# Decays of two tiles: bias inside a 128-row spreading product, exponentials of 512 columns

## The chip, the core and the metric

The kernel runs on one core of a Trainium2 chip. The core has a matmul engine (TensorE, PE in the profile), an elementwise engine (VectorE, DVE), an activation engine (ScalarE, ACT), a general one (GpSimd, POOL) and a queue engine that issues transfers (SyncE, SP). The metric is the device time in microseconds (us) of one execution. Before the change three runs took 531.83, 534.07 and 534.23 us; the median is 534.07.

## The reference, cut to what matters

Three layers follow one another on 4 batches of 768 positions. The first is a chunked linear attention with decays; its output feeds a gated feed-forward of width 1536 with RMS normalisation, and that one a second feed-forward of width 1024 with a shift by one position and a sigmoid gate.

```python
log_a = np.log(np.clip(a, 1e-06, 1.0))
for c in range(nc):
    cum = np.cumsum(la, axis=-1)
    L = np.exp(cum[:, :, :, None] - cum[:, :, None, :]) * causal
    CB = np.einsum('bhin,bhjn->bhij', Cc, Bc)
    y_intra = np.einsum('bhij,bhjd->bhid', CB * L, xc)
    y_inter = np.einsum('bhin,bhnd->bhid', Cc, state) * np.exp(cum)[..., None]
    state = decay_full * state + sum_j(B_j x_j decay_from_j)
...
xn = x / np.sqrt(np.mean(x * x, axis=-1, keepdims=True) + 1e-06) * rms_g
x = (silu(xn @ w_gate) * (xn @ w_val)) @ w_out
...
k = np.maximum(xk @ w_k, 0.0)
out = sigmoid(xr @ w_r) * ((k * k) @ w_v)
```

The matrix `L` is the "decays" of the title: for each batch and head a triangle of exponentials of differences of running sums of logarithms.

## The kernel before, in words

The sequence is cut into 6 tiles of 128 positions; with the 4 batches a tile has T = 512 columns. For each tile the kernel does the attention (8 heads, in chunks of 128 instead of 32), the normalisation, the first feed-forward (`ffn1`, 12 units of 128 channels, each with a gate product `g`, a value product `v` and, two units later, the contraction `x`) and the second one (`ffn2`, 8 units). A fp32 product is made of three products of rounded parts (`mm3`), so a unit of `ffn1` has 12 products before its contraction. The attention of tile t+1 is woven into the units of tile t by `hook`; that of tile 0 stands alone at the start, the prologue.

The weights come as 8-byte numbers and are turned into high and low parts on the chip, in pairs of jobs: ACT scales the two halves of the words (L257, L258), DVE clamps, merges twice and subtracts (L262, L267, L269, L279), and ACT rounds (L278). The first two pairs are converted in the prologue, the others among the units of tiles 0 and 1, from transfers into two staging buffers (`wst`).

Decays of tiles 0 and 1 are made by `sums_e`, `spread_e` and `exp_e`. `sums_e` takes the logarithm of `a` in 16 rows of 512 columns, sums along them with restarts (`starts`), keeps the rounded part and the rest as 32 + 32 rows of `sums`, and by four small products with `pick` brings the same sums into columns, with the sign turned (`cum`). For each batch and half (4 heads), `spread_e` makes in a PSUM tile `Eb` the sum of two products: an identity times a triangle of zeros and -30000 (`before`), and a row of `sums`, picked and spread over the 128 partitions. `exp_e` then takes four exponentials of 128 columns, each with its column of `cum` as the bias. Decays of the later tiles are made by scans over a loaded, spread copy of `a` (`load_e`, `e_scan`).

In the prologue, for each batch: `scores` makes the products of B and C in two PSUM tiles, `mask` multiplies them with the decays on DVE (`M`), `y_mm` makes the output and the state. After four batches the normalisation follows in two halves of columns (`rms_a`, `rms_b`, `xn_f`, `xn_split`), and with it the first products of `ffn1` can start. `decays` writes the clipped `a` to memory, twice, for the loads of later tiles.

The order in which each engine gets its instructions is not that of the code. The class `Order` takes all instructions with their dependences, holds a price for each kind, and lists them engine by engine in the order in which it would start them; this order is then fixed. A change in one place can therefore shift instructions on every engine. `WARM` sets two rows of products without use that keep PE busy (L749).

PE's products for the spread of a tile-1 batch go into the two buffers of the pool `at`, those of tile 0 into the four buffers of the pool `mm`, which `ffn1` uses as well for `g` and `v`. All exponentials of tile 1 stand before the table load for SiLU.

Of the kernel before, what the change touches and what calls it, by code (L numbers as in the profile page):

```python
# [16 lines left out]
P = 128  # L17
# [8 lines left out]
KW = 16  # L26
# [26 lines left out]
def shape_constants():  # L53
# [14 lines left out]
def tile_kernel(ctx: ExitStack, tc, a_c, x_t, B_t, B_s, C_s, B_p, C_p, C_h, kc,  # L68
# [73 lines left out]
    nc.gpsimd.memset(f32(pick), 0.0)
    for base in (0, -32):
        nc.gpsimd.affine_select(out=pick, in_=f32(pick), pattern=[[-1, RE]], base=base, channel_multiplier=1,
                                compare_op=ALU.not_equal, fill=1.0)
# [8 lines left out]
    cmask = wp.tile([P, NH * P], BF16, name="cmask")  # L154
    nc.gpsimd.memset(cmask, 0.0)
    nc.gpsimd.affine_select(out=cmask, in_=cmask, pattern=[[0, NH], [1, P]], base=0, channel_multiplier=-1,
                            compare_op=ALU.not_equal, fill=1.0)
    lmask = wp.tile([P, NB, P + 1], BF16, name="lmask")
    nc.gpsimd.memset(lmask, 0.0)
    nc.gpsimd.memset(lmask[:, :, 0:1], 1.0)  # L160

# [14 lines left out]


# [149 lines left out]
    sums = wp.tile([P, T], F32R, name="sums")  # L327
    cum = wp.tile([P, 4, RE], F32, name="cum")
    wp.tile([P, 48], F32, name="pad_m")

    def sums_e(a_sb):
        nc.vector.memset(f32(sums), 0.0)
        ln = t2("ln")[:RE]
        tabled(out=ln, in_=a_sb[:RE], func=AF.Ln)
        nc.vector.tensor_tensor_scan(out=ln, data0=starts.rearrange("p h i -> p (h i)"), data1=ln, initial=0.0,
                                     op0=ALU.mult, op1=ALU.add)
        nc.vector.tensor_copy(sums[:RE], ln)
        nc.vector.tensor_tensor(out=sums[32:32 + RE], in0=ln, in1=f32(sums[:RE]), op=ALU.subtract)
        ps = patt.tile([P, T], F32, tag="at", name="cumt")[:, :4 * RE].rearrange("p (h r) -> p h r", h=4)
        for h in range(4):  # L340
            mm = nc.tensor.matmul(ps[:, h], sums[:, h * P:(h + 1) * P], pick, start=True, stop=True)
# [428 lines left out]
    for b in range(NB):  # L770
# [14 lines left out]
        if b == 0:  # L785
            decays(a_sb)
# [390 lines left out]
```

## Time and profile before

| | |
|---|---|
| time, three runs | 531.83, 534.07, 534.23 us |
| span of the profiled execution | 532.1 us, 7505 instructions |
| its own time | listed nowhere apart from the three runs above |
| PE busy | 517.5 us (97%), 2831 products |
| DVE busy | 402.7 us (76%), 640 instructions |
| ACT busy | 314.7 us (59%), 546 instructions |
| POOL busy | 14.3 us (3%), 30 instructions |
| granted TensorE clock, mean | 0.994 of full speed |

The busy shares are means over the whole span. The prologue, up to about 31 us, and the units of tiles 0 and 1, up to about 150 us, have other limits than the rest, so the views by stretch and the rows in order of time are of more use than the table. A row of a timeline gives the start, the length, the line, and in brackets how long the engine had been idle before and what ended that. Instructions that follow each other overlap a little, so the distance of two starts is the time that one costs its engine.

### The profile page before, as it was taken

Reading aid. Unit: us, or ns where it says so; the run is one execution under the profiler, and the core shown is the slowest. Engines: PE = TensorE matmul, PEld = TensorE weight load, DVE = VectorE, ACT = ScalarE, POOL = GpSimd, SP = SyncE. Lnnn points to the kernel's source line nnn. Section 1 sums busy time; section 2 is a strip of 40 time slices with the busy share of each in tenths; the row PEclk is TensorE's granted clock in tenths of the full one; section 3 lists DMA queues with packets and bytes.
Section 4 is the critical chain, followed back from the end, with each engine's and each line's share of the span. In section 5 each row is a group of like instructions: output and inputs, shape, how many; then the busy total and the mean of one; then the engine's idle time right before and its main releaser. Section 6 shows DMA issues by size and latency. Waiting matters only on the chain.

```text
span 532.1 us, 7505 instructions
## 1 busy us (share of the span) xinstructions
PE 517.5 (97%) x2831; PEld 414.7 (78%) x2831; DVE 402.7 (76%) x640; ACT 314.7 (59%) x546; POOL 14.3 (3%) x30
## 2 busy tenths in 40 slices
PE   9969989999989999999999999999999999999997
PEld 6646767778768888888788888888888888888885
DVE  5798999999999986587996598986455863335772
ACT  4998768845736774445774445774437663245552
POOL 4000000000002000001000001000000000000000
PEclk9988999999999999999999999999999999999999
DMA  8543565534334011314011314011000010000001
GB/s 256 196 158 112 172 216 183 173 94 149 99 109 149 20 41 41 118 62 176 22 39 42 119 58 160 1 41 39 1 0 2 2 39 1 0 0 1 21 21 39
DMA packets 21635, 42.20 MB, mean 79 GB/s; under 512 B 2064, under 2 KB 4880, under 8 KB 21600
## 3 DMA queue, kind: packets, MB, share of 16 engines
q1 hardware_dynamic: 19296, 33.34, 18.8%
q10 hardware_dynamic: 2304, 8.39, 4.7%
q8 instruction: 22, 0.36, 0.3%
q14 instruction: 13, 0.11, 0.1%
HBM read 38.38 MB, written 3.34 MB: 78 GB/s over the span
## 4 chain that ended last, share of the span: by engine, by line
PE 89%; DVE 2%; ACT 2%; DMA 1%; issue 1%; ACTq 0%; DVEq 0%
PE v L625 10%; PE v L627 10%; PE v L626 10%; PE g L625 7%; PE g L626 6%; PE x L627 6%; PE g L627 6%; PE x L625 6%; PE x L626 6%; PE kp L625 4%; PE kp L627 4%; PE kp L626 4%; PE y L494 2%; PE y L523 1%; PE sc L462 1%; PE rps L626 1%
## 5 line engine op out<-in xcount | busy, mean ns | idle before, releaser
L656 DVE TENSOR_TENSOR hf<-sl,v 128x512 f32<-128x512 f32 x72 | 49.2, 683 | 48.8 <-PE v L627 45.2
L128 ACT CAST h<-hf 128x512 fp32r<-128x512 f32 x72 | 44.5, 618 | 62.7 <-DVE hf L656 58.5
L116 ACT ACTIVATE sl<-g 128x512 f32<-128x512 f32 x72 | 42.7, 593 | 44.5 <-PE g L627 44.4
L131 DVE TENSOR_TENSOR h<-hf,h 128x512 fp32r<-128x512 f32 x72 | 50.4, 702 | 23.4 <-ACT h L128 23.3
L625 PE MATMUL g<-xn,wgh 128*128 128x512 f32 x144 | 58.4, 409 | 1.5 <-ACT sl L116 0.8
L625 PE MATMUL x<-h,woh 128*128 128x512 f32 x144 | 56.5, 393 | 0.8 <-ACT h L128 0.8
L626 PE MATMUL g<-xn,wgl 128*128 128x512 f32 x144 | 57.2, 397 | 0.0
L625 PE MATMUL v<-xn,wvh 128*128 128x512 f32 x144 | 56.4, 395 | 0.6 <-ACT sl L116 0.6
L627 PE MATMUL g<-xn,wgh 128*128 128x512 f32 x144 | 56.9, 395 | 0.0
L626 PE MATMUL v<-xn,wvl 128*128 128x512 f32 x144 | 56.5, 392 | 0.0
L627 PE MATMUL v<-xn,wvh 128*128 128x512 f32 x144 | 56.3, 391 | 0.0
L627 PE MATMUL x<-h,woh 128*128 128x512 f32 x144 | 55.8, 391 | 0.4 <-DVE h L131 0.4
L626 PE MATMUL x<-h,wol 128*128 128x512 f32 x144 | 56.1, 389 | 0.0
L722 DVE TENSOR_TENSOR k<-rl 128x512 f32<-128x512 f32 x48 | 35.2, 738 | 15.1 <-ACT rl L721 14.9
L128 ACT CAST h<-k 128x512 fp32r<-128x512 f32 x48 | 29.7, 620 | 16.0 <-DVE k L722 15.9
L131 DVE TENSOR_TENSOR h<-k,h 128x512 fp32r<-128x512 f32 x48 | 32.7, 685 | 7.4 <-ACT h L128 7.0
L721 ACT ACTIVATE rl<-kp 128x512 f32<-128x512 f32 x48 | 28.4, 595 | 16.2 <-PE kp L627 15.8
L625 PE MATMUL kp<-xm,wkh 128*128 128x512 f32 x96 | 37.8, 393 | 0.0
L627 PE MATMUL v<-h,wvvh 128*128 128x512 f32 x96 | 37.5, 390 | 0.0
L627 PE MATMUL kp<-xm,wkh 128*128 128x512 f32 x96 | 37.5, 390 | 0.0
L625 PE MATMUL v<-h,wvvh 128*128 128x512 f32 x96 | 37.4, 389 | 0.0
L626 PE MATMUL v<-h,wvvl 128*128 128x512 f32 x96 | 37.4, 389 | 0.0
(135 smaller groups left out, 1040.7 us busy)
## 6 DMA issues: line engine op xcount, KB each, us to landing
E<-la_r ACTq DMA_DIRECT2D x16, 512.0 KB
x<-in_x_t SPq DMA_DIRECT2D x6, 512.0 KB
wst<-in_w_gate SPq DMA_DIRECT2D x6, 512.0 KB
wst<-in_w_val SPq DMA_DIRECT2D x6, 512.0 KB
wst<-in_w_out SPq DMA_DIRECT2D x6, 512.0 KB
Br<-in_B_s SPq DMA_DIRECT2D x12, 256.0 KB
Cr<-in_C_s SPq DMA_DIRECT2D x12, 256.0 KB
out<-r SPq DMA_DIRECT2D x12, 256.0 KB
```

Of the source, the lines that this page charges most:

```text
L116: ins.append(lambda: nc.scalar.activation(out=out, in_=in_, func=func, **kw))
L128: nc.scalar.copy(x[:, 0, :], src)
L131: last[0] = le.tensor_tensor(out=x[:, 1, :], in0=src, in1=f32(x[:, 0, :]), op=ALU.subtract).ins
L462: nc.tensor.matmul(bank[half][:, q * 256:(q + 1) * 256], bs[:, p, :], cs[:, p, :, :].rearrange("p a i -> p (a i)"), start=True, stop=True)
L494: nc.tensor.matmul(y[half][32 * j:32 * j + 32, at[half]:at[half] + P], x[:, b, h * D:(h + 1) * D], m[:, h, :], start=start and at[half] == ...
L523: mm = nc.tensor.matmul(y[half][:, k * P:(k + 1) * P], Sf[g, b + k].rearrange("p h d -> p (h d)"), d["Ch"][g, b + k, :], start=k == 0, sto ...
L625: nc.tensor.matmul(ps, w[0][:, k, ws], x[:, 0, :], start=first, stop=False)
L626: nc.tensor.matmul(ps, w[1][:, k, ws], x[:, 0, :], start=False, stop=False)
L627: nc.tensor.matmul(ps, w[0][:, k, ws], x[:, 1, :], start=False, stop=last)
L656: nc.vector.tensor_mul(hf, sl, v)
L721: nc.scalar.activation(out=rl, in_=kp, func=AF.Relu)
L722: nc.vector.tensor_mul(k2, rl, rl)
```

## The change

The logarithms are now made in 128 rows at once: `a` of a tile is loaded four times, into 128 rows of 128 columns (`load_a4`), clipped, taken to the logarithm and summed by a scan with ones. From the sums DVE makes two operands for PE with the help of constant columns that come with `k_sb` (`GL` to `MR`): `spread_l`, in which each batch and half has 128 columns for its rows, and `spread_r`, in which each head has 128 columns. One of the operands has the sums and ones, the other ones and the negative sums, each in rounded part and rest, so that their product over 128 rows is already the difference of the running sums. Nothing is left for a bias, and one exponential covers 512 columns. The operands lie in the tiles of `wk` and `wvv`, weights of the second feed-forward that are filled later.

`sums`, `cum`, `pick`, `starts` and the small products are gone. Both tiles' logarithms, and both `sums_e`, are called ahead of the first exponential. The load of `a` in 48 rows, for `decays`, comes after the first weight loads, its clip after the first batch. `k_sb` is loaded second instead of sixth. A tile of padding goes, and `carry` is taken later from its pool, so that the working tiles start at multiples of 512 bytes.

```diff
@@ constants @@
-KW = 16
+GL, SL, CL, SR, CR, ML, MR = 16, 17, 18, 19, 20, 21, 29
+KW = 33
...
+    rest, last, head = p % 4 % 2, p % 4 // 2, p // 4 % NH
+    k[:, GL] = np.where(rest == 1, -1.0, 0.0)
+    seq = p // 32
+    k[:, SL], k[:, CL] = np.where(last == 1, -1.0, 0.0), last == 0
+    k[:, SR], k[:, CR] = last == 0, last == 1
+    for j in range(8):
+        k[:, ML + j] = (seq == j // 2) & (head // 4 == j % 2)
+    for h in range(4):
+        k[:, MR + h] = head % 4 == h
@@ tile_kernel @@
-    starts = t2("starts", BF16)[:RE].rearrange("p (h i) -> p h i", h=4)
...
-    pick = wp.tile([P, RE], F32R, name="pick")
...
+    spread_l = [wk[0][:, c, :].rearrange("p (h j) -> p h j", h=8) for c in range(2)]
+    spread_r = [wvv[0][:, 2 * c:2 * c + 2, :].rearrange("p k (h i) -> p (k h) i", i=P) for c in range(2)]
@@ sums_e @@
-    sums = wp.tile([P, T], F32R, name="sums")
-    cum = wp.tile([P, 4, RE], F32, name="cum")
-    wp.tile([P, 48], F32, name="pad_m")
-    def sums_e(a_sb):
...
+    a4 = t2("a4").rearrange("p (c i) -> p c i", c=4)[:, :2]
+    def load_a4(c):
+        nc.sync.dma_start(out=a4[:, c], in_=a_c[c].unsqueeze(1).broadcast_to([32, 4, P]))
+    def logs_e(c):
+        clip(a4[:, c])
+        tabled(out=a4[:, c], in_=a4[:, c], func=AF.Ln)
+    def sums_e(c):
+        ln, w = a4[:, c], t2("hv", F32R)
+        hi, v = w[:, :P], w[:, P:2 * P]
+        nc.vector.tensor_tensor_scan(out=ln, data0=f32(ones), data1=ln, initial=0.0, op0=ALU.mult, op1=ALU.add)
+        nc.vector.tensor_copy(hi, ln)
+        nc.vector.scalar_tensor_tensor(out=v, in0=f32(hi), scalar=kcol(GL), in1=ln, op0=ALU.mult, op1=ALU.add)
+        def placed(f, to, m, n):
+            nc.vector.tensor_mul(to, f32(f).unsqueeze(1).broadcast_to([P, n, P]),
+                                 k_sb[:, m:m + n].unsqueeze(2).broadcast_to([P, n, P]))
+        right, left = w[:, 2 * P:3 * P], w[:, 3 * P:]
+        for f, sc, cc in ((right, SR, CR), (left, SL, CL)):
+            nc.vector.tensor_scalar(out=f, in0=f32(v), scalar1=kcol(sc), scalar2=kcol(cc), op0=ALU.mult, op1=ALU.add)
+        placed(right, spread_r[c], MR, 4)
+        for j, n in ((0, 2), (2, 6)):
+            placed(left, spread_l[c][:, j:j + n], ML + j, n)
@@ spread_e, exp_e @@
-            nc.tensor.matmul(ps, pick[:, r:r + 1].broadcast_to([P, P]), sums, start=False, stop=True)
+            nc.tensor.matmul(ps, spread_l[c][:, 2 * b + half], spread_r[c].rearrange("p h i -> p (h i)"),
+                             start=False, stop=True)
...
-        for h in range(4):
-            tabled(out=A[c]["E", b][:, 4 * half + h, :], in_=ps[:, h * P:(h + 1) * P], func=AF.Exp,
-                   bias=cum[:, h, c * NR + 2 * b + half:c * NR + 2 * b + half + 1])
+        tabled(out=A[c]["E", b][:, 4 * half:4 * half + 4, :].rearrange("p h i -> p (h i)"), in_=ps, func=AF.Exp)
@@ the start @@
+    load_a4(0)
+    nc.sync.dma_start(out=k_sb, in_=kc)
+    load_a4(1)
...
-    clip(a_sb)
-    cumt = sums_e(a_sb)
+    a_sb = load_a()
+    for c in range(2):
+        logs_e(c)
+    sums_e(0)
     spread_e(0, 0)
     scores(0, 0)
-    chains.append((cumt, groups[0][0]))
     spread_e(0, 1)
+    sums_e(1)
...
         if b == 0:
+            clip(a_sb)
             decays(a_sb)
```

The planner then orders anew. On DVE, in the prologue from the first mask on, the order before is this (`M` is the masked scores, `wt` and `wst` are weights in conversion, `state` and `Sf` the state of the attention):

```order
L481 TENSOR_TENSOR M<-sc,E 128x512 x4
L549 COPY state<-y 128x64
L553 TENSOR_TENSOR Sf<-state,k_sb 128x128
L481 TENSOR_TENSOR M<-sc,E 128x512 x2
L549 COPY state<-y 128x64
L553 TENSOR_TENSOR Sf<-state,k_sb 128x128
L481 TENSOR_TENSOR M<-sc,E 128x512 x2
L262 TENSOR_SCALAR wt_167<-wt_167 128x1024
L267 SCALAR_TENSOR_TENSOR wst_161<-wt_167,wst_161 128x1024
L549 COPY state<-y 128x64
L269 SCALAR_TENSOR_TENSOR wt_167<-wt_167,wst_161 128x1024
```

After the change the same place reads:

```order
L492 TENSOR_TENSOR M<-sc,E 128x512 x4
L266 TENSOR_SCALAR wt_152<-wt_152 128x1024
L560 COPY state<-y 128x64
L492 TENSOR_TENSOR M<-sc,E 128x512 x2
L271 SCALAR_TENSOR_TENSOR wst_146<-wt_152,wst_146 128x1024
L184 TENSOR_SCALAR a_sb<-a_sb 48x512
L196 COPY a_r<-a_sb 48x512
L197 MEMSET a_r 48x4
L560 COPY state<-y 128x64
L492 TENSOR_TENSOR M<-sc,E 128x512 x2
L273 SCALAR_TENSOR_TENSOR wt_152<-wt_152,wst_146 128x1024
```

The clamp and the merge of the first weight pair have moved in between the masks, and so have the clip of `a_sb` and its copy `a_r`; the products `Sf` have left.

On ACT, from the last exponential of tile 0 to the SiLU table, the order before is this (`xn` is the normalised input of `ffn1`, `rs` and `nw` its factors):

```order
L278 CAST wvh<-wt_167 128x2x256
L116 ACTIVATE rs<-ss,k_sb 128x256
L116 ACTIVATE rs<-rs 128x256
L116 ACTIVATE nw<-rs 128x256
L128 CAST xn<-xnf 128x256 x2
L116 ACTIVATE E<-Eb,cum 128x128 x7
L128 CAST xn<-xnf 128x256 x2
L116 ACTIVATE E<-Eb,cum 128x128
L258 ACTIVATE wst_418<-wst_418 128x1024
L116 ACTIVATE E<-Eb,cum 128x128
L257 ACTIVATE wt_457<-wst_418 128x1024
L116 ACTIVATE E<-Eb,cum 128x128
```

After the change:

```order
L126 ACTIVATE rs<-ss,k_sb 128x256
L126 ACTIVATE rs<-rs 128x256
L282 CAST wgh<-wt_153 128x2x256
L138 CAST xn<-xnf 128x256 x2
L126 ACTIVATE nw<-rs 128x256
L261 ACTIVATE wt_432<-wst_391 128x1024
L262 ACTIVATE wst_391<-wst_391 128x1024
L126 ACTIVATE E<-Eb 128x512
L138 CAST xn<-xnf 128x256 x2
L126 ACTIVATE E<-Eb 128x512 x4
L282 CAST wvh<-wt_432 128x2x256
L282 CAST woh<-wt_432 128x512
```

The two passes over the third weight pair (`wt_432`, `wst_391`) now stand ahead of the second pair of casts to `xn`; before (`wst_418`, `wt_457`) they stood behind it.

On SP, after the first weight loads, the order is now this (`la_d` and `la_r` are the copies of `a` in memory, `la` a load from one of them):

```order
L191 DMA a_sb<-in_a_c 48x512
L311 DMA Ch<-in_C_h 128x512
L399 DMA Cr<-in_C_p 64x512 x2
L397 DMA Br<-in_B_p 64x256 x2
L199 DMA la_d<-a_sb 48x512
L198 DMA la_r<-a_r 48x512
L307 DMA la<-la_d 128x1x128
L242 DMA wst_391<-in_w_val 128x2x512
L242 DMA wst_391<-in_w_out 128x2x512
L316 DMA Bt<-in_B_t 128x512
L319 DMA x<-in_x_t 128x1024
```

The two stores, which stood directly behind the first four weight loads, stand behind the loads `Cr` and `Br` of tile 1; the third pair's weight loads follow the first load of `la`, and the loads `Bt` and `x` follow them.

## Rows read from the trace of the kernel before

**Rows 1.** The page's first line.

```profile
span 532.1 us, 7505 instructions
```

**Rows 2.** Windows: busy us (count) of PE, weight loads, DVE, ACT, POOL; clock, DMA.

```profile
10.70:20.30 9.60, 9.44 (x102) 5.62 (x106) 6.13 (x13) 9.57 (x33) 1.65 (x4) 1.00 0.63 234
20.30:31.00 10.70, 6.08 (x62) 4.10 (x54) 10.01 (x21) 10.40 (x25) 0.00 (x0) 1.00 0.69 226
31.00:44.30 13.30, 11.70 (x43) 7.71 (x43) 13.27 (x23) 13.06 (x35) 0.00 (x0) 0.87 0.47 162
44.30:50.00 5.70, 5.70 (x18) 4.54 (x19) 3.60 (x7) 4.37 (x7) 0.00 (x0) 0.70 0.24 77
50.00:100.00 50.00, 48.58 (x309) 36.86 (x308) 48.83 (x71) 36.85 (x55) 0.11 (x1) 1.00 0.58 193
100.00:143.00 43.00, 43.00 (x264) 34.21 (x264) 42.30 (x65) 26.30 (x43) 0.00 (x0) 1.00 0.36 111
...
155.00:532.10 377.10, 373.20 (x1963) 307.41 (x1961) 260.62 (x419) 204.17 (x335) 7.43 (x6) 1.00 0.13 46
```

**Rows 3.** Windows, same columns, around the stretches at the lower clock.

```profile
31.00:34.30 3.30, 3.30 (x8) 2.31 (x9) 3.30 (x8) 3.30 (x7) 0.00 (x0) 0.50 0.02 6
...
44.70:48.00 3.30, 3.30 (x10) 2.53 (x9) 2.17 (x4) 2.58 (x6) 0.00 (x0) 0.50 0.34 119
48.10:50.00 1.90, 1.90 (x10) 1.54 (x9) 1.03 (x2) 1.30 (x2) 0.00 (x0) 1.00 0.00 0
```

**Rows 4.** Timeline of DVE: start, length, line, operation, idle before.

```profile
4.23 1.19 DVE L195 COPY a_r<-a_sb 48x512 f32<-48x512 f32 x1
...
10.73 0.69 DVE L481 TENSOR_TENSOR M<-sc,E 128x512 f32<-128x512 f32 x1 [1.32 <-PE sc L445]
...
14.15 1.29 DVE L481 TENSOR_TENSOR M<-sc,E 128x512 f32<-128x512 f32 x2 [1.88 <-PE sc L445]
...
15.61 0.29 DVE L553 TENSOR_TENSOR Sf<-state,k_sb 128x128 f32<-128x128 f32 x1
...
21.15 1.23 DVE L267 SCALAR_TENSOR_TENSOR wst<-wt,wst 128x1024 int32<-128x1024 int32 x1 [0.27 <-ACT wst L258]
...
48.97 0.69 DVE L656 TENSOR_TENSOR hf<-sl,v 128x512 f32<-128x512 f32 x1 [1.81 <-PE v L627]
```

**Rows 5.** Timeline of POOL at the start.

```profile
0.73 0.51 POOL L139 MEMSET starts<- 16x512 bf16 x1 [0.29 <-POOLq L1147]
...
1.94 0.21 POOL L148 MEMSET eye<- 128x128 bf16 x1
...
3.99 1.15 POOL L156 TENSOR_SCALAR_AFFINE_SELECT cmask<-cmask 128x1024 bf16<-128x1024 bf16 x1
```

**Rows 6.** Timeline of ACT.

```profile
9.38 5.26 ACT L116 ACTIVATE E<-Eb,cum 128x128 f32<-128x128 f32 x20 [4.52 <-PE Eb L351]
...
42.31 1.28 ACT L115 ACT_TABLE_LOAD   x1
43.60 0.60 ACT L116 ACTIVATE sl<-g 128x512 f32<-128x512 f32 x1
44.09 1.14 ACT L257 ACTIVATE wt<-wst 128x1024 f32<-128x1024 f32 x1
```

**Rows 7.** Timeline of PE.

```profile
7.62 1.04 PE L350 MATMUL Eb<-before,eye 128*128 128x512 bf16 x4
...
12.92 1.13 PE L445 MATMUL sc<-Cr,Br 32*128 32x256 f32 x8
...
30.98 0.79 PE L625 MATMUL g<-xn,wgh 128*128 128x512 f32 x1 [0.65 <-ACT xn L128]
...
44.25 0.52 PE L625 MATMUL g<-xn,wgh 128*128 128x512 f32 x1 [0.78 <-ACT sl L116]
```

**Rows 8.** Timeline of SP, and a row of the chain that ended last.

```profile
16.67 2.93 SPq L386 DMA_DIRECT2D Br<-in_B_p  x2
...
136.10 5.40 DMA Br<-in_B_s
```

More of the change, by code (lines that the diff above doesn't have):

```diff
@@ L136, in tile_kernel @@
     k_sb = wp.tile([P, KW + 6], F32, name="k_sb")
-    RE = 2 * 2 * NB
-    starts = t2("starts", BF16)[:RE].rearrange("p (h i) -> p h i", h=4)
-    nc.gpsimd.memset(starts, 1.0)
-    nc.gpsimd.memset(starts[:, :, 0:1], 0.0)
-    pick = wp.tile([P, RE], F32R, name="pick")
[L142 to L145, printed above, removed]
     eye = wp.tile([P, P], BF16, name="eye")
@@ L153, in tile_kernel @@
                             compare_op=ALU.is_ge, fill=-30000.0)
[L154 to L160, printed above, removed]
     def kcol(j):
@@ L174, in mu_rest @@
             nc.vector.tensor_scalar(out=om_v[j], in0=mu_v[j], scalar1=-1.0, scalar2=1.0, op0=ALU.mult, op1=ALU.add)
+    cmask = wp.tile([P, NH * P], BF16, name="cmask")
+    nc.gpsimd.memset(cmask, 0.0)
+    nc.gpsimd.affine_select(out=cmask, in_=cmask, pattern=[[0, NH], [1, P]], base=0, channel_multiplier=-1,
+                            compare_op=ALU.not_equal, fill=1.0)
+    lmask = wp.tile([P, NB, P + 1], BF16, name="lmask")
+    nc.gpsimd.memset(lmask, 0.0)
+    nc.gpsimd.memset(lmask[:, :, 0:1], 1.0)
     la_d = dp.tile([NC, NB, NH, P], F32, name="la_d")
@@ L322, in load_e @@
         )
-    sums = wp.tile([P, T], F32R, name="sums")
-    cum = wp.tile([P, 4, RE], F32, name="cum")
-    wp.tile([P, 48], F32, name="pad_m")
-    def sums_e(a_sb):
[L332 to L339, printed above, removed]
-        for h in range(4):
-            mm = nc.tensor.matmul(ps[:, h], sums[:, h * P:(h + 1) * P], pick, start=True, stop=True)
-        nc.vector.tensor_scalar(out=cum, in0=ps, scalar1=-1.0, scalar2=None, op0=ALU.mult)
-        return mm.ins.name
+    a4 = t2("a4").rearrange("p (c i) -> p c i", c=4)[:, :2]
[19 more added lines that the diff above has]
+            placed(left, spread_l[c][:, j:j + n], ML + j, n)
     def spread_e(c, b):
         for half in range(2):
-            r = c * NR + 2 * b + half
             pool, tag = (patt, "at") if c else (pmm, "mm")
@@ L667, in ffn1 @@
         return acc, tail
-    carry = [rp.tile([P, 2, NB], F32, tag="carry", bufs=2, name="carry")]
-    nc.vector.memset(carry[0], 0.0)
+    carry = [None]
     xm = {}
@@ L756, in tile_kernel @@
     load_c0(1)
-    nc.sync.dma_start(out=k_sb, in_=kc)
     load_x(0, 0)
@@ L797, in tile_kernel @@
     mu_rest()
+    carry[0] = rp.tile([P, 2, NB], F32, tag="carry", bufs=2, name="carry")
+    nc.vector.memset(carry[0], 0.0)
     for b in range(NB):
```

2 lines of the change are left out of this document (removed).

## Prediction

> **What bounds the kernel now.** I read the windows by stage first. TensorE (PE) is busy 373.2 of the 377.1 us after 155 us, and those matmuls don't change, so a gain must come before. VectorE (DVE) is busy 10.01 of 10.70 us in 20.3 to 31, 13.27 of 13.30 in 31 to 44.3, 48.83 of 50 and 42.30 of 43 up to 143 [rows 2]. ScalarE (ACT) is full from 10.7 to 44.3 (9.57 of 9.60, 10.40 of 10.70, 13.06 of 13.30), then at 61 to 74% [rows 2]. So two engines are full in the prologue and one, DVE, stays full to 143. From the first mask product at 10.73 to 143 DVE idles 3.5 + 0.7 + 0.0 + 2.1 + 1.2 + 0.7 = 8.2 us by the differences of these windows [rows 2]. That is the most that a shorter ACT queue can give back there, unless DVE's own work falls.
>
> Where it idles, the DVE rows tell [rows 4]: up to 20.3 it waits for the next batch's scores on PE (1.88 us before the mask at 14.15), and at 48.97 it waits 1.81 us for a value product. The second is a matter of the clock: the granted clock was 0.50 (the lower level, 1.2 GHz) in 31 to 34.3 and 44.7 to 48 [rows 3]. The first fall came after PE had waited until 30.98 for the normalised input, the second after a stretch in which its next gate product waited to 44.25 for the first SiLU, which came behind the exponentials and a table load [rows 6, 7].
>
> **The exponentials.** Before, 64 of 128 columns with a bias each; 20 in a row took 5.26 us, 0.26 each, so 64 take 16.8 us of ACT [rows 6]. After, 16 of 512 columns. A 512-column activation from PSUM shows in the SiLU: it starts at 43.60 and the next instruction at 44.09, 0.49 us [rows 6]; its whole length, 0.60, is the upper bound. 16 × 0.49 = 7.8 us, so ACT loses 9.0 us (7.2 at the upper bound): 4.5 in the first tile, 4.5 in the second. In the first tile eight exponentials from about 9.9 end at 13.8 instead of 19.0, and the first weight conversion follows at once.
>
> **The new preparation.** DVE now makes the two operands of the spreading product per tile: a copy, a scaled add, two scalings of 128 columns and three placings of 512, 256 and 768 columns. A 128x128 product took 0.29, and two 512-column masks 1.29 together, so that the second started 0.60 after the first [rows 4]; thus a set costs four times 0.2 to 0.29, then 0.6, 0.35 and 0.9, about 2.7 us; two sets with scans and clips, at 0.2 each, 6.2. The order puts both sets ahead of the first mask. What goes on DVE (a 512-column fill, a scan, a cast, a difference, the bias copy) all stood ahead of 10.7 too. The loads come first in the queue, so the work can begin near 3 us.
>
> Here GpSimd (POOL) matters. The copy of a at 4.23 took 1.19 us and ended 0.28 after POOL's 1.15 us select, which began at 3.99 [rows 4, 5]: one held the other up. In the change POOL starts with the identity at 0.73 instead of 1.94 [rows 5], so that select runs to about 3.9, over the first clip. I take 0.9 us for the wait: clip done near 4.0, both scans by 5.9, both sets by 10.9. Without it, 10.0. The Trainium skill ("SBUF — State Buffer", Who interferes with whom) says that DVE's two-port operations and GpSimd take a shared port pair exclusively, and that the later one blocks for the whole instruction. The 1.19 us copy agrees, and by that rule the masks start at 10.9; by a sharing of bandwidth they would start near 10.0.
>
> PE's first products don't move: 16 warm-ups fill it until the identity products at 7.62 [rows 7], then the scores, then the spreads, so the first exponential ends near 10.4. Masks thus start at 10.9 against 10.73: a loss of 0.2 (a gain of 0.3 without the port wait).
>
> **The mask loop.** Scores of a batch take both banks of their pool, and scores to mask is 12.92 to 14.15, 1.23 us [rows 4, 7]. Two masks take 1.29 [rows 4]. A batch therefore still takes some 2.5 us with exponentials for nothing, and the last mask ends near 20.3, as before. What changes is what DVE does in the bubbles: its order now has a clamp and a first merge of weights (0.6, taken like a mask, and the 1.2 of the merge at 21.15 [rows 4]) among the masks, possible because ACT gets to the weights 5 us earlier. Of the 3.5 us idle there, 1.3 stays (before the third mask), 0.5 is a new wait for ACT's first conversion, 1.7 goes.
>
> **What moves into the full stretch.** The clip of a and its copy leave the early, free time of DVE and stand among the masks. Alone, without POOL beside them, 512 columns of this kind should take what the copy took after POOL had ended, 0.28 to 0.35; two and a fill make 0.7 us lost. The bound is 1.31 + 1.19, seen with POOL beside them.
>
> **To the first gated product.** Up to the fourth normalised half DVE's order holds, against before, one more merge (1.2), four more weight subtractions (2.4), three fewer state products (-0.9) and those 0.7. It saves 4.2 - 1.8 = 2.4 us of idle time. So the first product comes at about 30.98 + 0.2 + 3.4 - 2.4 = 32.2, later by 1.2, but with 2.7 us of DVE work and some 3 us of ACT work already done.
>
> From there ACT has seven exponentials, two casts, one 1024-column pass and the 1.28 us table load before the first SiLU: 7 × 0.49 + 1.2 + 1.1 + 1.3 = 7.0, so SiLU near 39.5, with PE at half clock at first near 40.5, against 43.60. DVE has 7.3 us of work for 9 us and waits some 2.0 us for that SiLU: a new wait. At its first gate product (41.1 against 44.3, when SiLU had taken 0.60 from 43.60) it has 3.5 us less behind it than before (two scans, one product and two masks, less a clamp), so it is 0.3 behind; the fillers then serve in 44 to 50, where 2.1 us were idle.
>
> **The sum** on DVE, first mask to 143: idle before 8.2; after 1.3 + 0.5 + 2.0 + 1.9 for the rest (0.7 and 1.2 of the last windows) = 5.7. Gain 8.2 - 5.7 = 2.5, less 0.2 and 0.7: 1.6 us. The instruction counts of DVE up to the 19th gate product are otherwise the same in both orders, so a lead at 143 is the gain at the end. The profiled span is 532.1 [rows 1]; its own time is given nowhere apart from it; the runs shown are 531.83, 534.07 and 534.23, the median 2.0 above the span. The span should become 530.5, the median 532.5.
>
> Costed at nothing: the new spread product has the columns of the old; the scratch for the operands lies in weights of the second feed-forward, filled only after 90 us; the tiles moved to multiples of 512 bytes, since the mask (on such multiples) and the gate product (64 bytes short of one) both take 0.69 us (at 10.73 and 48.97 [rows 4]). If that cover is wrong it is a rate of every elementwise operation, and any sign.
>
> **Rival 1: PE is the bound, and the relief of ACT counts nearly whole.** Then what counts is the third unit's gate product, at 44.25 before [rows 7]. PE gets to it from 32.2 through 24 products (ten took 1.9 us at the full clock [rows 3]; 0.19 to 0.23 each, 5.2), eight spreads of two such products (3.4) and a batch of scores (1.13 [rows 7]): 41.9, or 43.4 if the clock falls once as before, since ten products take 3.3 us at the lower level and 1.9 at the upper [rows 3]. The second fall, another 1.4, goes. Gain 0.9 + 1.4 to 2.3 + 1.4; with the better end, as DVE's lead adds to it, 3.7: 530.4. For it: PE idles only 1.4 us in 50 to 100. Against: DVE idles less there, 1.2 [rows 2].
>
> **Rival 2, slower: loads behind a store.** ACT's order now has both 1024-column passes of the third weight pair ahead of the last two casts of the normalised input; before they stood behind. Their loads stand on SP behind a load of decays, which must wait until the store of the clipped a has landed, itself behind the second load of keys (before at 16.67 with 2.93 for two [rows 8]). So the store goes out near 19.6. A 256 KB load of the later stretch took 5.40 us on the chain [rows 8]. If the store lands in 2 us (assumed), weights are asked for near 22.5 and there near 28, when ACT gets to them at 28.6: no loss, my case. If store and weights take 5.4 and 8, a backlog as DMA is at 0.69 there [rows 2], they land near 33, the first product starts near 36, and DVE, whose last input splits stand in front of 13 further operations, idles 4.4 us more: 532.5 + 4.4 = 536.9. It decides from a landing later than 29. For it: all later loads on SP wait in line too. Against: the 0.69 came with the second tile's keys and x asked for ahead of these weights, and now the weights are asked for first.
>
> **Rival 3:** 0.60 an exponential, and the port wait or the copy at its upper bound: 0.5 to 1.8 us lost, 533.0 to 534.3; inside my own range.
>
> **Chances.** Mine (with rival 3) 0.50, 531.0 to 534.5; rival 1 0.28, from 529.0 to 531.4; rival 2 0.17; 0.05 for another order's luck downstream, both ways. 0.5% of 534.07 is 2.7 us, about what a measurement of this kernel tells from no change: faster means under 531.4, slower over 536.7. Faster: rival 1 but for a twentieth, and a tenth of mine, 0.33; slower: two thirds of rival 2 and most of the odd cases, 0.16; same 0.51. Range 529.0 to 536.7.
>
> **What would show it.** Right: exponentials of 512 columns 0.48 to 0.50 apart and the eighth over by 14; first mask at 10.5 to 11; masks 2.5 us apart; first SiLU at 39 to 41, a DVE wait of about 2 us for it; one fall of the clock, not two; DVE still full to 143. Wrong: a first product after 34 with ACT waiting for weights (rival 2); DVE with 3 us or more idle between 50 and 143 (rival 1); an elementwise operation with another duration (alignment).

## The result and the profile after

Five runs of the changed kernel took 535.76 to 536.69 us, median 535.98, against 533.41 before: ratio 1.0061, interval 1.0041 to 1.0082. In a later set of nine the median was 534.72, ratio 1.0042 (1.0021 to 1.0062). So the change is slower, by 0.4 to 0.6%; the forecast was 532.5, a little faster than before. The profiled execution took 536.01; its span, by the page's first line:

```profile
span 534.0 us, 7440 instructions
```

That is 1.9 us more than [rows 1]. The windows of [rows 2], after (PE, weight loads, DVE, ACT, POOL; clock, DMA share, GB/s):

```profile
10.70:20.30 9.60, 8.46 (x105) 5.09 (x104) 7.54 (x16) 8.78 (x15) 1.66 (x4) 1.00 0.78 271
20.30:31.00 10.70, 8.28 (x47) 4.99 (x48) 8.78 (x15) 5.59 (x13) 0.00 (x0) 0.84 0.76 238
31.00:44.30 13.30, 9.68 (x36) 6.24 (x35) 11.38 (x26) 11.36 (x20) 0.00 (x0) 0.87 0.47 160
44.30:50.00 5.70, 5.70 (x29) 4.28 (x28) 4.92 (x7) 5.69 (x10) 0.00 (x0) 1.00 0.34 94
50.00:100.00 50.00, 48.83 (x313) 36.53 (x313) 49.46 (x71) 34.46 (x53) 0.10 (x1) 1.00 0.62 194
100.00:143.00 43.00, 43.00 (x263) 34.76 (x262) 42.01 (x64) 25.51 (x41) 0.00 (x0) 1.00 0.34 104
```

ACT is relieved, as forecast: 5.59 instead of 10.40 us in 20.3 to 31. Yet DVE, 10.01 and 13.27 before, has 8.78 and 11.38 there: it waits more, not less. From the first mask to the first product of `ffn1`, before and after:

```profile
10.73:30.98 20.25, 15.47 (x155) 9.67 (x155) 16.12 (x33) 19.92 (x57) 1.65 (x4) 1.00 0.66 230
```
```profile
11.50:35.43 23.93, 16.75 (x152) 10.03 (x151) 19.77 (x39) 17.68 (x33) 1.59 (x4) 0.91 0.73 242
```

DVE works 3.65 us more in this stretch and idles as much as before, 4.16 us against 4.13. The forecast had 1.8 us of idle time there.

The clock is down three times instead of twice, around 21 to 24, 35 to 37 and 151 to 153:

```profile
21.00:24.00 3.00, 3.00 (x20) 1.57 (x20) 3.00 (x6) 1.14 (x2) 0.00 (x0) 0.50 0.49 93
35.00:37.00 2.00, 2.00 (x6) 1.00 (x4) 2.00 (x5) 1.67 (x4) 0.00 (x0) 0.50 0.00 0
151.00:153.00 2.00, 2.00 (x5) 1.29 (x5) 2.00 (x4) 1.14 (x3) 0.00 (x0) 0.50 0.61 161
```

DVE after, against [rows 4] (start, length, line, operation, idle before and its releaser): the clip and the two casts that begin the operand sets, the masks, the last state copy, the first gate product. Behind them stands POOL's select, which runs beside the first clip.

```profile
3.11 0.84 DVE L184 TENSOR_SCALAR a<-a 128x128 f32<-128x128 f32 x1 [2.10 <-DMA a<-in_a_c]
...
4.67 0.20 DVE L184 TENSOR_SCALAR a<-a 128x128 f32<-128x128 f32 x1
...
5.59 0.20 DVE L344 CAST hv<-a 128x128 fp32r<-128x128 f32 x1
...
8.54 0.22 DVE L344 CAST hv<-a 128x128 fp32r<-128x128 f32 x1
...
11.50 1.28 DVE L492 TENSOR_TENSOR M<-sc,E 128x512 f32<-128x512 f32 x2
14.52 1.29 DVE L492 TENSOR_TENSOR M<-sc,E 128x512 f32<-128x512 f32 x2 [1.74 <-PE sc L456]
...
19.12 0.42 DVE L184 TENSOR_SCALAR a_sb<-a_sb 48x512 f32<-48x512 f32 x1
19.57 0.42 DVE L196 COPY a_r<-a_sb 48x512 f32<-48x512 f32 x1
...
20.17 1.28 DVE L492 TENSOR_TENSOR M<-sc,E 128x512 f32<-128x512 f32 x2
...
25.91 0.23 DVE L560 COPY state<-y 128x64 f32<-128x64 f32 x1 [1.35 <-ACT yT L524]
...
44.97 0.69 DVE L667 TENSOR_TENSOR hf<-sl,v 128x512 f32<-128x512 f32 x1 [1.55 <-ACT sl L126]
```
```profile
2.78 1.09 POOL L173 TENSOR_SCALAR_AFFINE_SELECT cmask<-cmask 128x1024 bf16<-128x1024 bf16 x1
```

ACT after, against [rows 6]: the exponentials, the output copy `yT` of the last batch, the first SiLU.

```profile
10.26 4.03 ACT L126 ACTIVATE E<-Eb 128x512 f32<-128x512 f32 x8 [5.05 <-PE Eb L363]
...
25.51 0.37 ACT L524 COPY yT<-y 128x256 f32<-128x256 f32 x1 [1.75 <-PE y L511]
...
44.34 0.60 ACT L126 ACTIVATE sl<-g 128x512 f32<-128x512 f32 x1
```

PE after, the idle products at the start and then from the last masks to the first product of `ffn1` (`y` output and state products, `ss` mean square, `warm` products without use):

```profile
1.05 6.80 PE L759 MATMUL warm<-ones 128*128 128x512 f32 x16 [1.05 <-DVE carry L813]
...
21.00 0.66 PE L505 MATMUL y<-M,x 128*32 128x128 f32 x8 [1.28 <-DVE M L492]
21.59 2.07 PE L591 MATMUL ss<-sq,ones 128*128 128x256 f32 x4
23.59 0.66 PE L505 MATMUL y<-M,x 128*32 128x128 f32 x8
24.18 1.02 PE L759 MATMUL warm<-ones 128*128 128x512 f32 x3
25.12 0.32 PE L511 MATMUL y<-x,Bd 128*32 128x64 f32 x8
...
26.86 1.02 PE L591 MATMUL ss<-sq,ones 128*128 128x256 f32 x4
...
34.62 0.58 PE L362 MATMUL Eb<-before,eye 128*128 128x512 bf16 x1 [5.34 <-ACT E L126]
...
35.43 0.71 PE L636 MATMUL g<-xn,wgh 128*128 128x512 f32 x1
```

And before, in the same place, on PE and on ACT:

```profile
20.45 0.62 PE L494 MATMUL y<-M,x 128*32 128x128 f32 x16
20.88 0.29 PE L500 MATMUL y<-x,Bd 128*32 128x64 f32 x8
21.11 2.56 PE L749 MATMUL warm<-ones 128*128 128x512 f32 x10
```
```profile
22.34 0.35 ACT L513 COPY yT<-y 128x256 f32<-128x256 f32 x1
```

Before, the last state product came 0.6 us after the last masks (20.28) and `yT` 2.06 after them. After, the masks end at 21.45. Behind them PE does the `ss` of the first half, the second value products and three idle products before that state product, and up to about 24.3 it does so at 1.2 GHz: the four `ss` take 2.07 us, the same four 1.02 at 2.4 GHz (at 26.86). `yT` comes 4.06 after the masks, and the first product is at 35.43, not 32.2.

So the first product is 4.45 us later than before: 1.17 up to the end of the masks, 2.00 from there to `yT`, and 1.28 behind `yT`, where DVE has more work up to the product. In the 2.00 two causes act together, the order on PE and its clock; exps128_held below tells them apart.

### The profile page after: what moved, and what is told of

Read it like the earlier page. It is cut to its first block, busy times and chain, and to the rows that moved or that the text cites. A ratio compares the mean times of both kernels' runs of the same rounds, so it can differ in the third digit from the quotient of the medians.

```text
span 534.0 us, 7440 instructions
## 1 busy us (share of the span) xinstructions
PE 517.7 (97%) x2827; PEld 414.1 (78%) x2827; DVE 405.8 (76%) x653; ACT 306.3 (57%) x499; POOL 13.3 (2%) x25
## 4 chain that ended last, share of the span: by engine, by line
PE 71%; DVE 1%; ACT 0%; issue 0%; DVEq 0%
PE v L638 8%; PE v L636 8%; PE v L637 8%; PE x L636 5%; PE x L638 5%; PE x L637 5%; PE g L636 4%; PE g L637 4%; PE g L638 4%; PE kp L636 4%; PE kp L638 4%; PE kp L637 4%; PE y L505 1%; PE sc L473 1%; PE rps L636 1%; PE rps L637 1%
## 5 line engine op out<-in xcount | busy, mean ns | idle before, releaser
L637 PE MATMUL kp<-xm,wkl 128*128 128x512 f32 x96 | 37.3, 389 | 0.0
```

Source lines behind the costliest of these rows:

```text
L637: nc.tensor.matmul(ps, w[1][:, k, ws], x[:, 0, :], start=False, stop=False)
```

## What the end hangs on

For every kernel that ran, the table has the times of five events in the profiled execution: the last masks over, the last `yT`, the first product of `ffn1`, the first SiLU, and the 24th gate product on DVE (in tile 1; from there it is some 370 us to the end of the span in all of them); then the distance from `yT` to it, the time of that one execution, the median of all runs and their mean granted clock.

| kernel | masks | yT | product | SiLU | gate 24 | yT to it | its time | median | clock |
|---|---|---|---|---|---|---|---|---|---|
| before | 20.28 | 22.34 | 30.98 | 43.60 | 161.40 | 139.06 | – | 533.2 | 0.993 |
| after | 21.45 | 25.51 | 35.43 | 44.34 | 163.69 | 138.18 | 536.01 | 535.98 | 0.988 |
| after_rep | 21.33 | 25.33 | 35.27 | 44.14 | 163.48 | 138.15 | 535.59 | 534.72 | 0.989 |
| pad448 | 21.26 | 25.26 | 35.18 | 44.02 | 163.33 | 138.07 | 535.65 | 535.83 | 0.988 |
| noclip_held | 20.80 | 25.61 | 35.53 | 44.93 | 163.69 | 138.08 | 535.87 | 535.27 | 0.989 |
| noprep_held | 21.04 | 25.78 | 35.70 | 45.03 | 163.72 | 137.94 | 535.84 | 535.48 | 0.990 |
| clip_off | 20.46 | 23.76 | 33.70 | 43.35 | 162.28 | 138.52 | 534.67 | 534.77 | 0.989 |
| prep_act | 20.20 | 22.54 | 32.52 | 41.23 | 160.50 | 137.96 | 532.39 | 533.59 | 0.990 |
| sums1_b0 | 22.07 | 26.89 | 37.24 | 46.87 | 165.63 | 138.74 | 537.58 | 536.00 | 0.986 |
| y_first | 20.76 | 22.97 | 33.23 | 41.91 | 161.13 | 138.16 | 533.27 | 534.27 | 0.988 |
| best | 19.91 | 24.72 | 34.85 | 46.74 | 162.89 | 138.17 | 534.96 | 534.97 | 0.986 |
| best_a | 20.71 | 24.74 | 34.51 | 46.12 | 162.14 | 137.40 | 533.94 | 535.33 | 0.986 |
| warm_last | 21.08 | 24.87 | 36.07 | 45.92 | 166.21 | 141.34 | 538.31 | 533.78 | 0.990 |
| warm32 | 21.45 | 26.25 | 36.10 | 44.65 | 163.38 | 137.13 | 535.49 | 534.33 | 0.994 |
| prep_warm32 | 21.98 | 26.27 | 36.34 | 44.88 | 163.38 | 137.11 | 535.22 | 533.01 | 0.996 |
| exps128 | 20.83 | 22.98 | 31.68 | 45.75 | 163.78 | 140.80 | 536.22 | 536.21 | 0.990 |
| exps128_held | 22.08 | 24.69 | 34.53 | 45.01 | 164.00 | 139.31 | 536.35 | 537.22 | 0.989 |
| best_warm32 | 20.52 | 24.07 | 33.54 | 43.34 | 159.44 | 135.37 | 531.60 | 532.68 | 0.995 |
| best_y_warm24 | 20.24 | 22.27 | 33.26 | 43.20 | 159.30 | 137.03 | 531.37 | 531.51 | 0.992 |
| before_warm28 | 19.60 | 21.68 | 30.32 | 43.97 | 161.74 | 140.06 | 534.12 | 532.96 | 0.999 |

In the eleven rows from after to best_a the distance is 137.4 to 138.7, while `yT` itself lies anywhere from 22.5 to 26.9. The row warm_last, with the same eleven idle products, does not fit (141.34); its profiled execution took 4.5 us more than its median. The change shortened the distance by 0.9 and made `yT` 3.2 late: +2.3 at the 24th gate product.

A single profile says which wait is there. The medians, which mix executions with more and fewer stretches at the lower clock, follow more weakly: among the runs of one and the same program 0.003 of the mean clock goes with some 0.8 us (slope over all runs, each program about its own mean). An estimate with this slope: the means of the change's fourteen runs (535.6 us at 0.989) and of the kernel before (533.1 at 0.993, 133 runs) differ by 2.5 us, of which half goes with the clock and half would be left at equal clock. It is no clean split, since a fall of the clock in the mask loop also delays `yT`.

## The experiments

Theories: A, DVE sets the pace, so its start, work and idle time from the first mask add up; B, the short exponentials are worth what was forecast and other parts cost more; C, the late last masks; D, alignment; E, idle time fills what work leaves; F, the falls of the clock; G, the end follows the last `yT`. A run called held keeps the changed kernel's order on the engines that the edit leaves alone; most others are planned anew.

**Exponentials of 128 again, planned anew and in the changed order.**

```diff
-        tabled(out=A[c]["E", b][:, 4 * half:4 * half + 4, :].rearrange("p h i -> p (h i)"), in_=ps, func=AF.Exp)
+        for h in range(4): tabled(out=A[c]["E", b][:, 4 * half + h, :], in_=ps[:, h * P:(h + 1) * P], func=AF.Exp)
```

> The changed kernel (535.98 us) with one part undone: each exponential of 512 columns is split into four of 128 again (no bias), and the order is planned anew. ACT gets back about 48 x 0.2 = 9 us of work. Theory A (DVE sets the pace to 155 us; the shorter ACT queue bought nothing net, because the first product of the feed-forward came late anyway): 535.5 to 537.5, and DVE idle from first mask to the 20th gate product 8 to 9.5 us, as in the change (8.25) and before (8.14). Rival B (the ACT saving is worth what was forecast and the rest of the change costs more than it looks): the 2.5 us come on top, 538 to 540.

> The same split of the exponentials, but planned with the price of the long ones, so that DVE, POOL and SP keep the changed kernel's order word for word and only ACT gets longer by about 9 us. It measures what that order owes to the short exponentials. Theory A: the order was made for the short ones, so the weight conversions in the mask loop and the first SiLU (44.34) come 4 us later and DVE waits for them: 539 to 543. Rival B' (ACT is nowhere on the path): within 0.7 us of 535.98.

Planned anew 536.21, ratio 1.0062 (1.0042 to 1.0082), as the change: B falls. In the held order 537.22, ratio 1.0082 (1.0060 to 1.0105): 1.2 to 2.5 us over the change's two medians, so neither the 3 to 7 of A nor the nothing of its rival. The trace of the first tells more. With four exponentials in place of each one of 512 columns ACT reaches the weights later, PE's last batch isn't held up (copy 2.15 us after the masks), and `yT` is 2.5 us earlier than in the change:

```profile
22.98 0.37 ACT L524 COPY yT<-y 128x256 f32<-128x256 f32 x1 [0.77 <-PE y L511]
...
45.75 0.60 ACT L126 ACTIVATE sl<-g 128x512 f32<-128x512 f32 x1
```

but the SiLU is 1.4 later (44.34 in the change), and the 24th gate product comes as in the change. So in these two profiles the prologue takes back, ahead of `yT`, what the 512-column exponentials give behind it.

The trace of the second settles what the order on PE costs by itself. PE's order behind the last masks (over at 22.08) is that of the change, but in 21 to 25 the granted clock is 1.00:

```profile
21.62 0.42 PE L505 MATMUL y<-M,x 128*32 128x128 f32 x8 [1.28 <-DVE M L492]
21.98 1.13 PE L591 MATMUL ss<-sq,ones 128*128 128x256 f32 x4
23.04 0.43 PE L505 MATMUL y<-M,x 128*32 128x128 f32 x8
23.40 0.98 PE L759 MATMUL warm<-ones 128*128 128x512 f32 x3
24.30 0.32 PE L511 MATMUL y<-x,Bd 128*32 128x64 f32 x8
```
```profile
24.69 0.37 ACT L524 COPY yT<-y 128x256 f32<-128x256 f32 x1 [0.31 <-PE y L511]
```

Here `yT` follows the masks by 2.61 us. With the clock down for part of the stretch it is 4.0 to 4.1 (after, after_rep, pad448); with the clock down for all of it, 4.7 to 4.8 (noclip_held, noprep_held, warm32). Before it was 2.06, with ACT's weight pass rather than PE ahead of the copy. So of the change's 2.00 us behind the masks the order alone makes some 0.55, and some 1.45 come in because PE is at 1.2 GHz there.

**The clip and the copy cut to 4 columns, the rest of the order held; and both off DVE.**

```diff
-            clip(a_sb)
+            clip(a_sb[:, :4])
-        nc.vector.tensor_copy(a_r, a_sb)
+        nc.vector.tensor_copy(a_r[:, :4], a_sb[:, :4])
```
```diff
-            clip(a_sb)
+            clip(a_sb, nc.gpsimd)
-        nc.vector.tensor_copy(a_r, a_sb)
+        nc.scalar.copy(a_r, a_sb)
```

> The changed kernel in its own order, with the clip of a_sb and the copy a_r cut from 512 to 4 columns (left out: the clip of the rest, and the zeros in the copy; both stores read a_sb as loaded). It prices the clip and the copy among the masks, 0.42 + 0.42 on DVE. Theory A (DVE path): the last masks come 0.7 to 0.8 us earlier and the end 0.5 to 0.9 us, 535.1 to 535.5. Rival C (the clip makes the last masks late, PE idles, its clock falls at 21, and the last batch is late by 2 us for it): the clock stays at 1.00 in 21 to 24.5, the first product comes 2 us or more earlier than 35.43, and the end comes 1.5 us or more earlier, under 534.5.

> The changed kernel with the clip of a_sb on POOL, the copy a_r on ACT and the zeros on POOL: 0.95 us of DVE work among the masks is gone, nothing is left out; DVE's order is otherwise the changed one but for a few neighbours swapped. Theory A (DVE's work and idle time from the first mask to 160 us add up to the end): 535.0 to 535.4. Rival C (late last masks, clock fall at 21, late last batch): under 534.5, with the first product before 34. Rival E (DVE's idle time grows by as much as its work shrinks, because masks and the last batch wait for PE and ACT anyway): 535.7 to 536.3.

noclip_held: 535.27, ratio 1.0034 (1.0016 to 1.0052), a median that A allows. In its profile the last masks end 0.65 earlier, `yT` does not (25.61), the 24th gate product neither (163.69), which speaks against A; but here the clock was at 0.50 from 18.6 to 25.4, longer than in the change, so this one execution does not decide. C's forecast fails, as the clock still fell. clip_off: 534.77, 1.0040 (1.0023 to 1.0057), between the forecasts of A and C; the planner orders PE anew and `yT` is 1.75 earlier, the gate product 1.4.

**The second operand set: cut to 4 columns in the changed order, called later, or partly on ACT.**

```diff
+        n_ = 4 if c else P
-        nc.vector.tensor_copy(hi, ln)
+        nc.vector.tensor_copy(hi[:, :n_], ln[:, :n_])
...
```
```diff
     spread_e(0, 1)
-    sums_e(1)
...
+        if b == 0:
+            sums_e(1)
```
```diff
-        nc.vector.tensor_copy(hi, ln)
+        (nc.scalar.copy if c else nc.vector.tensor_copy)(hi, ln)
+            if c: nc.scalar.activation(out=f, in_=f32(v), func=AF.Identity, scale=kcol(sc), bias=kcol(cc))
```

> The changed kernel in its own order, with the second operand set cut from 128 to 4 columns of each block (left out: the operands of tile 1; tile 1 gets the decays of tile 0). 2.4 us of DVE work ahead of the first mask is gone and nothing else. Theory A (that preparation is what costs at equal clock): first mask at 10.8 to 11.0 instead of 11.5, end 0.5 to 1.2 us earlier, 533.8 to 534.5 by the median beside 535 to 535.8 of the change. If the first mask waits for PE and ACT anyway and its start does not reach the end: no difference.

> The changed kernel with sums_e of tile 1 called after the first batch instead of ahead of the first exponential: nothing is taken off DVE, but the placings of tile 1 (1.8 us of the 2.95) go behind the first two masks. Theory A (what counts is that DVE's preparation stood ahead of the first mask, while DVE idles 2 us among the masks): first mask at 10.8 or before, idle time in the mask loop under 1 us, end 1 to 2 us earlier, 533.9 to 535, most of what the step on ACT gave. If that step counted by the 0.75 us that it took off DVE: 535.7 to 536.3.

> The changed kernel with the cast and the two scalings of tile 1's operands on ACT (0.75 us of DVE work less), which the plan then places between the exponentials; tile 1's placings go behind the first masks. Theory A: first mask at 10.8 instead of 11.5, and 0.5 to 1.0 us less at the end: 535.0 to 535.5. Rival E: the first mask is earlier but the time is as before, 535.7 to 536.3.

noprep_held is the clearest miss of A: 2.4 us of DVE work less, the first mask 1.34 earlier (10.16), the last masks over only 0.41 earlier, and `yT` later than in the change, since on PE the same products stand ahead of the last state product, here all at 1.2 GHz:

```profile
21.17 2.08 PE L592 MATMUL ss<-sq,ones 128*128 128x256 f32 x4
23.18 0.65 PE L506 MATMUL y<-M,x 128*32 128x128 f32 x8
23.76 1.65 PE L760 MATMUL warm<-ones 128*128 128x512 f32 x3
25.34 0.36 PE L512 MATMUL y<-x,Bd 128*32 128x64 f32 x8
```

DVE idles 5.8 us from its first mask to the first product, against 4.2 in the change: the work taken off became waiting. The median was 535.48 (1.0020 to 1.0055), not the 533.8 to 534.5 of A. sums1_b0 did not gain (536.00), prep_act did, more than A could explain (533.59, 1.0017, 0.9998 to 1.0036): the first has `yT` at 26.89, the second at 22.54.

**Paddings; the change once more.** Two tiles of 448 and 64 bytes around the first `t2`.

> The changed kernel with two paddings that put the working tiles back to 448 above a multiple of 512 bytes, as before; all other tiles stay on multiples and the order is the same on every engine. All my theories: no difference, 535.6 to 536.4, elementwise durations the same to 0.01 us. Rival D (the alignment costs or gains a rate): every 512-column operation changes by the same share, 1% of DVE's 406 us would be 1 to 4 us.

> The changed kernel itself once more, beside the others on one chip: the mark that they are compared with. All theories: 535.0 to 536.5. It also tells how the time of one and the same program goes with the mean granted clock of its run; from the runs so far, one fall of 3.4 us (0.0033 of the mean) goes with about 1.1 us.

pad448: 535.83; the 72 gate products take 682 ns on average with the tiles at 448 and at 0. D falls. after_rep: 534.72, a little below what was expected, at mean clocks of 0.980 to 0.994 with 538.70 at the lowest and 533.86 at the highest.

**The idle products.** First behind the last state product, then 32 in place of 11.

```diff
+            if last_st[0] is not None:
+                chains.append((last_st[0].ins.name, mm.ins.name))
```
```diff
-WARM = (16, 11)
+WARM = (16, 32)
```

> The changed kernel with one more ordering: the idle products of the second row (11) only after the last state product, ahead of which three of them stood (24.18 to 25.12). Rival C (the last batch's products on PE are what counts): yT of the last batch 1 us earlier than 25.51, first product at 34.5 or before, end 1 us or more earlier, under 535. Theory A: the first product may come earlier, the end stays, 535.6 to 536.4.

> The changed kernel with 21 more idle products on PE (32 instead of 11), which the plan puts into the 5.3 us in which PE waits for the normalised input; DVE, ACT and SP keep the changed order word for word. Theory F (the loss is the falls of the clock: the change has three of 3.4 us in its profile, the kernel before two): the fall at 34.5 goes, the first SiLU comes 1 to 1.5 us earlier, and the end 1 us or more, 534 to 535. Theory A (DVE's start, work and idle time): DVE waits 1.5 us for that SiLU, so it counts too, but the later end of the wait is hidden in part: 535 to 536.

> The kernel before with 17 more idle products on PE (28 instead of 11), placed in its wait of 4 us before the first gated product; the orders of DVE and ACT change at some seven neighbours. Theory F (each fall of the clock costs about 1 us, and falls follow such waits): falls per execution from 2.0 to about 1, time 532 to 532.6 against 533.1. If falls only cost where they add to a late prologue: no difference.

warm_last: 533.78 (1.0013 to 1.0052). The median is under the 535 that C forecast, but the plan put a spreading product of tile 1 into the gap, and `yT` came at 24.87 and the first product at 36.07, in a profile with a span of 536.3, far over the median. It decides nothing. In warm32 the clock is up where PE had waited 5.3 us before:

```profile
35.00:37.00 2.00, 1.35 (x5) 0.49 (x4) 1.97 (x6) 1.72 (x5) 0.00 (x0) 1.00 0.01 3
```

and the distance from `yT` falls by 1.0, to 137.13. But in this execution the clock was down from 19.3 to 26.1, `yT` came 0.7 later, and the gate product only 0.3 earlier; the median is 534.33 (1.0005 to 1.0037). In the kernel before, 28 idle products in place of 11 raise the mean clock from 0.993 to 0.999 and change nothing: 532.96, ratio 1.0001 (0.9990 to 1.0012). There ACT is full up to the SiLU [rows 2], which would hide PE's clock; that this is the reason was not tested. So F holds in the changed kernel in part: a fall costs where PE is the engine that the others wait for, as behind the last masks, and it has no one price.

**PE's last batch alone.** The second value product and the state product ahead of `ss` and of the idle products; the other engines keep the changed order (`behind` holds the `ss` products; the idle products are chained as above, and so are the spreading products of tile 1).

```diff
+        if b == NB - 1:
+            chains.extend((last_st[0].ins.name, m) for m in behind)
```

> The changed kernel with one thing moved, on PE alone: the last batch's second value product and state product now stand ahead of the first mean-square product and of the idle products, behind which they stood (21.59 to 25.12). DVE, ACT and SP keep the changed order word for word. Theory G (the end follows the last output copy yT): that copy at 23.2 to 23.8 instead of 25.3 to 25.5, the first product at 33.2 to 33.8 instead of 35.4, the 24th gate product 1.5 to 2 us earlier, time 533 to 534 beside 534.7 to 536 of the change. Theory A (DVE's work counts, from the first mask): the copy moves, the end does not, 535 to 536.

```profile
1.05 5.57 PE L765 MATMUL warm<-ones 128*128 128x512 f32 x16 [1.05 <-DVE carry L823]
...
20.31 0.93 PE L507 MATMUL y<-M,x 128*32 128x128 f32 x16 [1.27 <-DVE M L494]
21.06 0.29 PE L515 MATMUL y<-x,Bd 128*32 128x64 f32 x8
21.28 1.74 PE L595 MATMUL ss<-sq,ones 128*128 128x256 f32 x4
```
```profile
22.97 0.36 ACT L528 COPY yT<-y 128x256 f32<-128x256 f32 x1
```

`yT` is 2.54 us earlier than in the change, and product, SiLU and gate 24 move with it, by 2.2, 2.4 and 2.6: that the end follows `yT`, theory G, is right in the trace. Not all of the 2.54 is the order's, though. The masks are 0.7 earlier: the sixteen idle products at the start took 5.57 us in this execution and 6.80 in the profile of the change, and DVE waits 1.05 us instead of 1.74 for the second batch's scores. From the masks to `yT` it is 2.21 instead of 4.06, and here the clock fell only at about 21.7, behind the state product; against the same stretch of exps128_held, also at the full clock (2.61), the move gains 0.4.

The runs show less: median 534.27, 1.0034 (1.0017 to 1.0052), just over G's 533 to 534, with mean clocks of 0.980 to 0.997. The interval overlaps that of after_rep, so by the medians the move is not shown to gain. By the means, brought to one clock with the slope above, y_first lies 1.0 us under the change's fourteen runs (standard error 0.3) and 0.2 over the kernel before; this is an estimate.

**Versions.** best: clip, copy and tile 1's cast and scalings off DVE as above, also tile 0's state copies on ACT and tile 1's `Bd` on POOL. best_a leaves the last two out.

> Clip and copy off DVE and tile 1's cast and scalings on ACT as in the two runs above, and also the four state copies of tile 0 on ACT (4 x 0.13 to 0.22) and the four products Bd of tile 1 on POOL (1.1 us of DVE by 0.27 each): some 3 us of DVE work less in all, in place of the 9 us that ACT was relieved of. Theory A: 2 to 3.5 us less than the change, 532.5 to 534, at or a little under the kernel before (533.41). Rival E: 535 to 536.

> Clip on POOL, copy on ACT, and tile 1's cast and scalings on ACT: the two single steps that each gave something (1.2 and 2.4 us) together. Theory A: they add, 532 to 533, under the kernel before. Rival E (each only reshuffles the waits): 533.6 to 535.

> Tile 1's cast and scalings on ACT (533.6) and 32 idle products in the second row, in the order of that run on DVE, ACT and SP. Theory F: falls from 3.0 to about 1.5 per execution, 532 to 533, at or under the kernel before. Otherwise 533.5 to 534.5.

> The version with 3 us less DVE work (clip and copy, tile 1's cast and scalings, state copies and Bd off DVE; 535.0 with 4.5 falls per execution) and 32 idle products, in its own order. Theory F: that version lost its gain to falls; with some two fewer 532.5 to 533.5. If its loss is DVE waiting for ACT and POOL instead: 534.5 to 535.5.

> The version that beat the kernel before (532.4 on the mean, 3 us less DVE work and more idle products) with the same move of the last batch's products on PE, and 24 instead of 32 idle products. Theory G: its copy yT from 24.1 to 22.5 to 23, the time 531 to 532, 0.2 to 0.4% under the kernel before. Theory A: 532.2 to 532.8.

best 534.97 (1.0024 to 1.0056), best_a 535.33 (1.0022 to 1.0050), both over what A forecast (532.5 to 534 and 532 to 533). The parts do not add; their `yT` are at 24.72 and 24.74. prep_warm32 533.01 (0.9986 to 1.0018), level with the kernel before. best_warm32 532.68, ratio 0.9985 (0.9972 to 0.9998), and with PE's last batch first, best_y_warm24, 531.51, ratio 0.9973 (0.9961 to 0.9985), within G's forecast and outside A's. Both lie a little under the kernel before, by 0.15 and 0.27%. Taking work off DVE alone gave little; with PE kept busy and its last batch first it is 3.2 to 4.5 us against the change's two medians. The two parts of that last step, PE's order and 24 instead of 32 idle products, were not run apart.

## Why the prediction was wrong

- *The exponentials.* Right: 8 in 4.03 us, 0.50 apart, over at 14.29, 0.3 later than the sign asked for; the mask loop did not get shorter by them, as said.
- *The new preparation.* Mis-sized: a set takes 2.95 us (5.59 to 8.54 to 11.50), not 2.5 to 2.7, so the first mask came at 11.50, not 10.9. The wait for POOL was there: the clip beside the select took 0.84 us and ended at 3.95, 0.08 after it (forecast near 4.0); the next clip took 0.20. This agrees with the rule of the Trainium skill ("SBUF — State Buffer", Who interferes with whom) that the prediction quotes.
- *The mask loop.* Last masks over at 21.45, not 20.3: clip, copy and merge (0.95 and 1.22) stand ahead of the last two, whose scores were there at 19.3. Clip and copy cost 0.95, forecast 0.7.
- *To the first gated product: the step that failed.* The prediction took 2.4 us of idle time off DVE ("4.2 - 1.8") against 3.4 us of added work, "so the first product comes at about ... 32.2". Its 1.8 were all in the mask loop; for the stretch behind the last masks it put DVE's waiting at nothing, without a reason. The work came out as forecast (3.65), but the idle time did not shrink: 4.16 us, 2.06 up to the end of the last masks and 2.10 behind it, where DVE waits for the last batch's output (1.35 before the last state copy). That output comes through PE, which has other products ahead of it and runs at 1.2 GHz. So the product came 4.45 us later and not 1.2: 0.77 for the first mask, 3.65 of work, 0.03 of idle time. noprep_held shows it from the other side: its first mask is 1.34 us earlier, DVE idles 1.6 us more, and the product is no earlier (35.70).
- *From there.* The SiLU came 8.9 us after the product (forecast 8.3). DVE waited 1.55 us for it and 0.82 before that for a weight pass of ACT (forecast 2.0 for the SiLU). "One fall of the clock, not two" was wrong: three.
- *The sum.* To the 24th gate product, DVE starts 0.8 later, works 0.9 more and idles 0.6 more than before, against 0.2, 0.7 and -2.5. That such a sum comes out is bookkeeping: a DVE that is full after 50 us only hands on the lead with which it starts.
- *The rivals.* Rival 2 did not happen, though the first product did come after 34: ACT's pass over the third pair starts without a wait, at 31.97 (28.6 was taken). Rival 1 was further off in time (530.4), yet right that PE can be the engine that counts: in the prologue it was, and ACT, relieved as forecast, waited for PE there (1.75 us before the last `yT`). Alignment cost nothing.

Shown in the profiles: the idle time that did not shrink, the distance from `yT`, and the two things that hold `yT` up, PE's order and its clock behind the last masks. Shown by runs: that taking the second operand set off DVE gains nothing (noprep_held). Not settled: how much of the median's 1.5 to 2.6 us is the copy and how much the lower mean clock, beyond the estimate above, since both move together from one execution to the next; and why the clock falls in the mask loop in most profiles of the changed order and in none of the kernel before.

## What to carry to other kernels

Where an engine is full later, look for the one event from which the rest keeps its distance, and follow the chain through all engines to it; work taken off the full engine ahead of that event can be worth nothing. A shorter stage lets a scheduler pull other work forward, so ask what it puts in front of the last step of the chain, idle products included; here four products ahead of it took 1.02 us at the upper clock and 2.07 at the lower. Compare two reorderings over many executions and read the chain in the trace, since one median of five can be off by a microsecond.

## What was not expected of the hardware

PE's clock fell to 1.2 GHz by 21 us, in the mask loop, after waits of only 0.39, 0.17 and 1.28 us; ahead of the fall by 35 the wait was 5.34. The same products from the last masks to `yT` took 2.61 us at the full clock and 4.7 to 4.8 at the lower one. And one program's executions differ in how often the clock falls: the changed kernel's mean clock ranged from 0.980 (538.70 us) to 0.994 (533.86). Even the sixteen idle products at the start, the same in all versions, took from 5.26 (prep_act) to 6.80 us (after) in the profiles, with the granted clock shown as 1.00 throughout; why is open.
